# Real parts of eight squarings and the coefficient sums moved from VectorE to float32 matmuls with the identity

## The chip, the cores and the metric

The kernel runs on one core of one Trainium2 chip. The metric is the time of one execution on the device in microseconds (us). In the profile the engines are named PE (TensorE: matmuls; PEld: its weight loads), DVE (VectorE), ACT (ScalarE), POOL (GpSimd) and SP (SyncE, which here only issues DMAs). On each engine instructions run in the order in which the program lists them.

## The reference

Two layers, A and B, are applied twice in turn to one sequence of 2048 rows of 512 values (bfloat16), each on the normalised rows and with the input added back:

```python
x = A_x
x = x + _A_ref(_layernorm(x, axis=-1), A_wqkv, A_wo)
x = x + _B_ref(_layernorm(x, axis=-1), B_A_re, B_A_im, ...)
x = x + _A_ref(_layernorm(x, axis=-1), A_wqkv, A_wo)
x = x + _B_ref(_layernorm(x, axis=-1), B_A_re, B_A_im, ...)
```

A is attention with 32 heads of 16 over a window of 8 positions with step 2. B is a long convolution of every channel d with a filter K of 2048 taps, done with Fourier transforms. The filter is made from a diagonal state-space model with 128 states per channel:

```python
logdA = dt * A                 # A, Bc, Cc complex, [512, 128]; dt = exp(log_dt)
dB = dt * Bc
P = jnp.exp(logdA[:, :, None] * l[None, None, :])        # l = 0 .. 2047
K = jnp.einsum("dn,dnl,dn->dl", Cc, P, dB).real
```

The filter is the same for both B layers and is made once. This is the kernel generation, the part that is changed.

## The kernel before

The kernel generation is the function `k_gen`. States lie on the 128 partitions; the 512 channels lie along the free dimension, so that one real plane is a tile of 128 x 512 float32. It works with z = exp(dt A) and its powers z^(2^k):

- In the head, the six parameter arrays are loaded (`raw`), turned by PE into PSUM (`turned_by`, tiles `pt`, four of them in turn), and z is made as a real and an imaginary plane (`sq_z`).
- Eleven squarings (k = 0 to 10) give z^2 to z^2048. `square` (letter `s`, L1078) lets ACT square both planes into `ws`; `double` (L1082) lets DVE make the imaginary plane 2 re im; `differ` (L1085) lets DVE make the real plane by subtracting the two squares. Calls of `i` take `double` and `differ` in turn, k by k.
- `power` (`b`, L1096 and L1098) copies a power as bfloat16 into a table of factors: powers 3 to 7 into `Pw` (`pow_t`), the others into `Bt` (`B_t`). For powers 3 to 7 a further `b` writes the negated imaginary plane (L1102 on ACT, for power 5 L1104 on DVE), and `c` copies the real plane once more by DMA (`power_copy`, L1107).
- `c_part` (`C`) makes the coefficients C dB: for the real and for the imaginary plane two products (`t1`, `t2`) and their difference or sum, into `c0` (`c_t`), all on DVE (L1110).
- `b_part` (`M`) fills `B_t` by complex products on DVE: with 1536 or 1024 columns, and adds with 512. It needs the powers 0, 1, 2, 8, 9 and 10.
- `levels` (`T` and `U`) builds four chunks of a table `A_t` from the coefficients on DVE, in five levels of doubling size, level n with the power 3 + n; `T` makes chunks 0 and 2, `U` chunks 1 and 3, and `H` begins a chunk.
- `product` (`p`, L1268) multiplies `A_t` with `B_t` on PE, and ACT copies the result to `kgs` (`x`, L1276). After the last one, `k_store` writes the filter to device memory.

Woven into this is the front of the first attention layer: the loads of x (`d`), the statistics of its rows on ACT (`a`) and DVE (`3`), the normalising (`l`, `W`, `y`, `z`), the transposes on PE (`t`, L1196) with their copies on ACT (`e`), the projections on PE (`k`, `q`, L1206) with their copies on ACT (`K`, `Q`), and the first products of the logits (`X`, `Z`, `o`, `E`). `G` and `w` make the constants of the Fourier transforms and store them.

The order of all this is written out by hand: `ORDERK` is a text of 368 letters, and a loop takes the next call of the list that belongs to each letter. So the order of the letters is the order of each engine's instructions. The engine of some copies stands in `ENGK`. The other stages have texts of their own (`ORDER0`, `ORDERF`, `ORDER1`, `CORE0`, `CORE1`).

The framework adds the waits between engines from what the instructions read and write; tiles of a pool with several buffers are taken in turn, and a new one waits for the users of the old.

Of the kernel before, what the change touches and what calls it, by code (L numbers as in the profile page):

```python
# [20 lines left out]
P = 128  # L21
# [13 lines left out]
N = 128  # L35
# [8 lines left out]
DQT = 8  # L44
NQT = DQG // DQT
ORDERK = """
isCbCiCbsiMaiCCbsiMiGGsbcCbMaTMiiMisMbiMbsGbMiGbiMTbcsibTTaiTcbTsbMTiiGbTGGsTMGciaiMTGMcabMGMaTM
asaMMGMlalTiWMlaaiyTbayiyTMawaMytatMTelkaeMsqMkdliqMaMKMaMMqMqWMlbQQMMMqMyHykUUakpKkyyttkaxUUpKU
kaUUUUaqUUxeUQppqHkdxxKUqeQTkTaUTklqT3paTqlKWTkQTplqkyqx3Ty3QKxT3TTpqlkTpyyHqWEUxktQlKtkUzkekeTK
zUUUkkzkUztKkKtkkTUpexUUKUEkUkeUkUKpKUokxkpxpKUkUxxkqUKEpxoqkkUpUUxopXXXKQpZxxZZ  # L50
"""
ORDER0 = """
KD KA KA KA KD KA KD KA KD KA KD kA KA kD KA KD UA KD UA UA UD KA kA kD kA UD
UA UD UA kD kA kD u UD u u UA m m m UA u u UD u UA m kD UA kD UA m
m u UA u m kA u kD u m kD u kD kA kA yA m YA m yD u yA u m m m
u u yA m m u YA m yA w000D yD yA YD yA w010D YA yD yA
"""
LATE0 = "a s t g r b m"
ORDERF = """
yA h00 YA h01 v100A v110D h10 a0 z12A p0 z11A n0D h11 w001A w011A S a1 p1 T0 E01A z13A E00D n1G H2  # L60
P02 a2 P00 Q00 p2 T1 E10D E11D P01 P11 P12 n2D H3 a3 P13 T2 P10 E20D E21D P03 p3 P21 P22 n3D
P23 T3 E30D E31A P20 x1
"""
ORDER1 = """
UA UD UA UD UA UA UD UA UD UD u u m m u u m m UA u UA UD m UA u u
UD UA u m m u u m m u YD m u YA YA m u yD m yA u u m m u w001A
m m yA yA w000D YA yD yA YD w011D yA yD w010D yA yD yA v101A v103D v113A v102D v112D v111D v110A v100A
"""

CORE0 = """  # L70
# [914 lines left out]
NIA = 32  # L985
CH = 32
NROW = 641


def k_gen(tc, nc, a_consts, ins, kd, la, x_v, lnst, zero, b_consts):  # L990

    B_L = (0, 1, 2, 3, 4, 5, 6, 7, 256, 258, 260, 262, 512, 516, 768, 772, 1024, 1280, 1536, 1792, 2048)
    NCH = P // CH
    with ExitStack() as ctx:
        pw = ctx.enter_context(tc.tile_pool(name="kg_pow", bufs=1))
        Bt = pw.tile([P, 2, P, NB, 4], BF16, name="B_t")
        Pw = pw.tile([P, NCH, 5, 4, 4 * CH], BF16, name="pow_t")
        c0 = pw.tile([P, 2, 4 * P], BF16, name="c_t")
        tab = [ctx.enter_context(tc.tile_pool(name="kg_tab0", bufs=1))]
        c_psum, c_small = ExitStack(), ExitStack()  # L1000
        sp = c_small.enter_context(tc.tile_pool(name="kg_small", bufs=1))
        pst = c_psum.enter_context(tc.tile_pool(name="kg_ps_t", bufs=4, space=PSUM))
        late = {}
        iotas, a_rest = a_consts(sp)
        ident = la.c["ident"]
        la.front_open()
        la.front_psum()
        xb, ln, lvar, xps, pps = {}, {}, {}, {}, {}
# [10 lines left out]
        raw = {}  # L1019
        for name in ("A_im", "A_re", "B_re", "B_im", "C_re", "C_im"):  # L1020
            raw[name] = sp.tile([P, 4, N], BF16, name="raw_" + name)
            nc.sync.dma_start(raw[name][:], ins[name].rearrange("(t p) n -> p t n", p=P))
        x_load(0)
        zero()
        x_load(1)
# [29 lines left out]
        cur = {0: sp.tile([P, 2, 4 * P], F32, name="sq_z", tag="sq_z", bufs=2)}  # L1055
        a_re, turn = cur[0][:, 0], ws[:, 2]
# [12 lines left out]
        T = {name: turned_by(name, by_dt if name[0] == "C" else plain) for name in ("B_re", "B_im", "C_re", "C_im")}  # L1069
        for name, copy in (("B_re", nc.scalar.copy), ("B_im", nc.scalar.copy)):  # L1070
            b = sp.tile([P, 4 * P], BF16, name="in_" + name)
            copy(nat(b[:]), T[name])
            T[name] = nat(b[:])
        nc.vector.tensor_tensor(cur[0][:, 1], a_re, sn, ALU.mult)
        nc.vector.tensor_tensor(cur[0][:, 0], a_re, cs, ALU.mult)

        def square(k):
            nc.scalar.activation(ws[:, 0:2], cur[k][:], ACT.Square)  # L1078

        def double(k):  # L1080
            cur[k + 1] = sp.tile([P, 2, 4 * P], F32, name="sq_z", tag="sq_z", bufs=2)
            nc.vector.scalar_tensor_tensor(cur[k + 1][:, 1], cur[k][:, 0], 2.0, cur[k][:, 1], ALU.mult, ALU.mult)  # L1082

        def differ(k):
            nc.vector.tensor_tensor(cur[k + 1][:, 0], ws[:, 0], ws[:, 1], ALU.subtract)  # L1085

        def planes(k):
            return cur[k][:].rearrange("p r (c x) -> p r c x", c=NCH)

        def copy_by(eng):  # L1090
            return nc.scalar.copy if eng == "A" else nc.vector.tensor_copy

        def power(k):
            copy = copy_by(ENGK["b"][k + max(0, min(k - 3, 5))])
            if 3 <= k <= 7:
                copy(Pw[:, :, k - 3, 1::2, :].rearrange("p c r x -> p r c x"), planes(k))  # L1096
            else:
                copy(Bt[:, :, :, B_L.index(1 << k), :], cur[k][:].rearrange("p r (q g) -> p r q g", g=4))  # L1098

        def power_neg(k):  # L1100
            if ENGK["b"][2 * k - 2] == "A":
                nc.scalar.mul(Pw[:, :, k - 3, 2, :], planes(k)[:, 1], -1.0)  # L1102
            else:
                nc.vector.tensor_scalar(Pw[:, :, k - 3, 2, :], planes(k)[:, 1], -1.0, None, ALU.mult)  # L1104

        def power_copy(k):
            nc.sync.dma_start(Pw[:, :, k, 0, :], Pw[:, :, k, 1, :])  # L1107
# [1 line left out]
        def tt(*args):  # L1109
            return lambda: nc.vector.tensor_tensor(*args)  # L1110

        def c_part():
            for q, (x0, y0, x1, y1, op) in enumerate((("C_re", "B_re", "C_im", "B_im", ALU.subtract),
                                                      ("C_re", "B_im", "C_im", "B_re", ALU.add))):
                yield tt(nat(t1[:]), T[x0], T[y0], ALU.mult)
                yield tt(nat(t2[:]), T[x1], T[y1], ALU.mult)
                yield tt(c0[:, q], t1[:], t2[:], op)

        def bmul(src, by, dst):
            s0, s1, st = src  # L1120
# [258 lines left out]
def kernel(  # L1379
# [200 lines left out]
```

## Time and profile before

| | |
|---|---|
| median of 3 runs | 403.94 us (403.01 to 404.91) |
| span of the profiled execution | 402.6 us (its own time is not given) |
| DVE busy | 383.5 us, 95% of the span |
| PE busy (matmuls) | 328.0 us, 81% |
| ACT busy | 321.8 us, 80% |
| POOL busy | 59.1 us, 15% |
| DVE's last instruction of the kernel generation (L295) | ends at 110.7 us |
| k_store's 24 DMAs | issued from 110.01 us on |

The profile is of one execution; its span runs from the first instruction to the last. A row of the timeline has the start, the time, the engine, the line, the operation, the tile written, the tiles read and the shapes; in brackets stands how long the engine sat idle before, and what ended that. A row of the groups has the count, the busy time in us, the mean in ns and the idle time before. A row of a window has the length, the busy time of the engines with the number of instructions, the granted clock of TensorE, the share of time in which the DMA engines were busy, and GB/s. The two rows of digits show the span in 40 slices of 10.1 us, each digit the busy share in tenths.

### The profile page before, as it was taken

Reading aid. Unit: us, or ns where it says so; the run is one execution under the profiler, and the core shown is the slowest. Engines: PE = TensorE matmul, PEld = TensorE weight load, DVE = VectorE, ACT = ScalarE, POOL = GpSimd, SP = SyncE. Lnnn points to the kernel's source line nnn. Section 1 sums busy time; section 2 is a strip of 40 time slices with the busy share of each in tenths; the row PEclk is TensorE's granted clock in tenths of the full one; section 3 lists DMA queues with packets and bytes.
Section 4 is the critical chain, followed back from the end, with each engine's and each line's share of the span. In section 5 each row is a group of like instructions: output and inputs, shape, how many; then the busy total and the mean of one; then the engine's idle time right before and its main releaser. Section 6 shows DMA issues by size and latency. Waiting matters only on the chain.

```text
span 402.6 us, 14781 instructions
## 1 busy us (share of the span) xinstructions
PE 328.0 (81%) x6527; PEld 230.3 (57%) x6527; DVE 383.5 (95%) x460; ACT 321.8 (80%) x557; POOL 59.1 (15%) x75
## 2 busy tenths in 40 slices
PE   3000059999999989999998889999999998997895
PEld 2000026657735656756987888543456666566885
DVE  6999999999999999999999998979899999989994
ACT  7999888898656578988999987674666677989974
POOL 9402400000199500200600000100000001000000
PEclk9999997999999999999999999999999999999999
DMA  7952711115013875259236685730063019504606
GB/s 219 395 143 37 81 52 50 44 27 117 3 43 76 214 210 160 55 173 384 93 112 232 228 285 166 280 114 2 0 170 94 3 39 383 161 2 134 186 14 202
DMA packets 62323, 54.17 MB, mean 135 GB/s; under 512 B 33869, under 2 KB 50738, under 8 KB 60978
## 3 DMA queue, kind: packets, MB, share of 16 engines
q1 hardware_dynamic: 62250, 53.22, 43.5%
q8 instruction: 51, 0.84, 0.9%
q14 instruction: 14, 0.11, 0.1%
q10 hardware_dynamic: 8, 0.00, 0.0%
HBM read 30.15 MB, written 13.24 MB: 108 GB/s over the span
## 4 chain that ended last, share of the span: by engine, by line
PE 36%; DVE 31%; ACT 17%; issue 8%; DMA 5%; SPq 2%; POOL 1%; DVEq 0%; ACTq 0%; POOLq 0%
DVE pav L467 11%; PE pq L398 6%; PE pk L1268 5%; ACT a1s L791 5%; PE pp L1206 4%; DVE t L847 3%; PE pq L223 3%; DVE prod L342 3%; PE pp L282 3%; PE L L350 2%; ACT ub L860 2%; DVE B_t L1110 2%; DVE sq_z L1085 2%; DMA v_ext<-v_ext 2%; DMA kf_ring<-kf_dram 2%
## 5 line engine op out<-in xcount | busy, mean ns | idle before, releaser
L467 DVE TENSOR_TENSOR pav<-attn,v_ext 128x4096 bf16<-128x4096 bf16 (+1 forms) x34 | 72.4, 2168 | 0.4 <-DMA v_ext<-v_ext 0.3
L342 DVE TENSOR_TENSOR prod<-qT,kT_ext 128x4096 bf16<-128x4096 bf16 x29 | 67.0, 2341 | 1.4 <-PE L L350 0.9
L1196 PE MATMUL pt<-ident,x_blk 128*128 128x128 bf16 x64 | 5.9, 241 | 42.8 <-DVE x_blk L197 38.6
L1110 DVE TENSOR_TENSOR A_t<-A_t,pow_t 128x1024 bf16<-128x1024 bf16 (+4 forms) x46 | 38.3, 870 | 0.3
L492 PEld LDWEIGHTS <-pav 64*128 64x128 bf16 x1664 | 26.2, 95 | 13.5 <-DVE pav L467 8.6
L503 PE MATMUL pq<-wop,oT 128*128 128x512 bf16 x128 | 32.9, 379 | 0.7 <-ACT oT L494 0.7
L860 ACT CAST ub<-pb 128x1024 bf16<-128x1024 f32 x32 | 32.1, 1079 | 1.2 <-PE pb L809 1.2
L492 PE MATMUL po<-ident,pav 64*128 64x64 bf16 x1664 | 29.3, 190 | 4.2 <-DVE pav L467 3.2
L400 ACT CAST v_ext<-pq 128x512 bf16<-128x512 f32 x32 | 18.8, 586 | 16.2 <-PE pq L398 16.2
L809 PE MATMUL pb<-a1s,w_sb 128*128 128x64 bf16 x768 | 27.4, 193 | 5.0 <-ACT a1s L791 1.7
L398 PE MATMUL pq<-wv,xnT 128*128 128x512 bf16 x128 | 30.6, 380 | 0.0
L1206 PE MATMUL pp<-xnT,kT_ext 128*128 128x512 bf16 x96 | 27.1, 411 | 4.3 <-ACT kT_ext L1211 2.3
L1196 PEld LDWEIGHTS <-x_blk 128*128 128x128 bf16 x64 | 4.6, 107 | 44.8 <-DVE x_blk L197 38.8
L809 PEld LDWEIGHTS <-w_sb 128*128 128x128 bf16 x768 | 24.9, 98 | 7.2 <-issue 5.2
L791 ACT CAST a1s<-pb 128x1024 bf16<-128x1024 f32 x29 | 28.2, 1059 | 0.8 <-PE pb L802 0.8
L1268 PEld LDWEIGHTS <-A_t 128*64 128x64 bf16 (+1 forms) x512 | 22.9, 107 | 4.5 <-DVE B_t L1110 0.3
L1268 PE MATMUL pk<-B_t,A_t 128*64 128x84 bf16 (+1 forms) x512 | 24.6, 206 | 0.0
L791 DVE CAST a1s<-pb 128x1024 bf16<-128x1024 f32 x19 | 22.6, 1217 | 1.4 <-PE pb L802 1.3
L223 PE MATMUL pq<-xnT,kT_ext 128*128 128x512 bf16 x96 | 23.9, 380 | 0.0
L225 ACT CAST qT<-pq 128x512 bf16<-128x512 f32 x24 | 14.1, 586 | 9.3 <-PE pq L223 9.2
L509 ACT ACTIVATE x_sb<-pq 128x512 bf16<-128x512 f32 x24 | 14.3, 594 | 8.7 <-PE pq L503 8.7
L398 PEld LDWEIGHTS <-xnT 128*128 128x128 bf16 x128 | 11.6, 98 | 15.3 <-issue 3.0
(259 smaller groups left out, 897.0 us busy)
## 6 DMA issues: line engine op xcount, KB each, us to landing
w_sb<-w_dram SPq DMA_DIRECT2D x8, 1024.0 KB, 7.8
w_dram<-xnT SPq DMA_DIRECT2D x1, 4096.0 KB
kf_ring<-kf_dram SPq DMA_DIRECT2D x13, 256.0 KB, 4.8
kf_ring<-kf_dram SPq DMA_DIRECT2D x26, 128.0 KB, 4.3
v_ext<-v_ext SPq DMA_DIRECT2D x4, 784.0 KB, 6.6
x_blk<-in_A_x_dram SPq DMA_DIRECT2D x4, 512.0 KB, 4.1
kT_ext<-in_A_wqkv_dram SPq DMA_DIRECT2D x4, 512.0 KB, 9.2
x_sb<-in_A_x_dram SPq DMA_DIRECT2D x4, 512.0 KB, 5.3
```

The lines of the kernel that those rows point to most:

```text
L223: nc.tensor.matmul(pq[:], lhsT=self.wqk[:, dt, ft * P:(ft + 1) * P], rhs=self.xnT[:, dt, q * 512:(q + 1) * 512], start=(dt == 0), stop=(dt ...
L342: nc.vector.tensor_tensor(pr, self.qT[q][:, ft].unsqueeze(1).to_broadcast([P, W, 4, P]), kap, ALU.mult)
L398: nc.tensor.matmul(pp[:], lhsT=xnT[:, dt, a * P:(a + 1) * P], rhs=wv[:, dt, :], start=(dt == 0), stop=(dt == NDT - 1))
L467: nc.vector.tensor_tensor(pv[:, i], attn[:, n % 4].unsqueeze(2).to_broadcast([P, W, DH // parts, H]), vap, ALU.mult)
L492: nc.tensor.matmul(po[:, h, 0, i * nt + ft, :], lhsT=pvf[rows, i, w, ft * P:(ft + 1) * P], rhs=ident[rows, rows], start=(w == 0 and ft + i ...
L503: nc.tensor.matmul(pw[:], lhsT=oT[:, ftp, :], rhs=self.wo[:, ftp, :], start=False, stop=(ftp == NDT - 1))
L791: (self.nc.scalar.copy if eng == "act" else self.nc.vector.tensor_copy)(dst, src)
L809: nc.tensor.matmul(p2[:, j, :], lhsT=self.w2[:, ec * EC + j, :], rhs=a1s[:, ec * EC + j, :], start=True, stop=True)
L860: nc.scalar.copy(ub[:], p2)
L1110: return lambda: nc.vector.tensor_tensor(*args)
L1206: nc.tensor.matmul(pps[kind, b, ft][:], lhsT=la.wqk[:, dt, c:c + P], rhs=la.xnT[:, dt, b * 512:(b + 1) * 512], start=(dt == 0), stop=(dt = ...
L1268: nc.tensor.matmul(o, lhsT=lhs, rhs=Bt[:, ri, c * CH + ql].rearrange("p b g -> p (b g)"), start=(not half and j % 4 == 0 and ri == 0), sto ...
```

## The change

- `k_gen` makes two float32 identities, `ident32` and `nident32` (the negated one), from `ident` by DVE at its start.
- `differ` for k = 3 to 10 no longer runs on DVE: PE adds the two squares up in a PSUM tile by two float32 matmuls, one with the identity and one with the negated identity. The real plane of the powers 4 to 11 then stays in PSUM (a tile of the pool of `pt`) and is read from there by `square`, `double` and `power`. The imaginary plane has a tile of its own, so ACT's squares and power copies of k = 4 and up are made plane by plane, 512 columns each.
- The difference and the sum in `c_part` are made in the same way by PE, and copied to `c0` by ACT. The second pair of products has tiles of its own, in room of `kT` that is not yet used.
- The `raw` tiles lie in the room of `qT`.
- `ORDERK` has the same 368 letters in another order. The other order texts differ only in their line breaks.

The diff, cut to this:

```diff
+sibCCiisbisCCCiiMMbsGiCMMiMMbbMMsTbGiiscbbccMMbiTisbTTbGGGcGTTTiTTGiiTTTsGbibbGGGasTcMMMMaiiaaaa
+aasMMTiillWaTlbyMMwMyyayMMaMMMbattseeMMMiiMMMMkkMMMMMkkbKHqqKaqqppaaQadxaUUUUUUUkkllxUWppaQUUKlq
+UqyUUUqqyyHyQxttkkTTTTTpdeeKTTTTQT3qqqqaaQkkQaakkKTaallqxqpWEQx333KxlTTykkkppTkyyyxxHtUUeKUUtppl
+kUUeUKkxkkUWpUlzKzzzxkkttKkeKekpUUUUUKkkkkUUUEUUxUKEqxppKooxqXkxkQpKkkoXXKpZZZxx
...
+SQ_PE = 3
...
+        ident32 = sp.tile([P, P], F32, name="ident32")
+        nident32 = sp.tile([P, P], F32, name="nident32")
+        nc.vector.tensor_copy(ident32[:], ident[:])
+        nc.vector.tensor_scalar(nident32[:], ident[:], -1.0, None, ALU.mult)
...
         def square(k):
-            nc.scalar.activation(ws[:, 0:2], cur[k][:], ACT.Square)
+            if k <= SQ_PE:
+                nc.scalar.activation(ws[:, 0:2], (im[k] or z0)[:], ACT.Square)
+                return
+            for r in range(2):
+                nc.scalar.activation(ws[:, r], cur[k][r], ACT.Square)
 
         def double(k):
-            cur[k + 1] = sp.tile([P, 2, 4 * P], F32, name="sq_z", tag="sq_z", bufs=2)
-            nc.vector.scalar_tensor_tensor(cur[k + 1][:, 1], cur[k][:, 0], 2.0, cur[k][:, 1], ALU.mult, ALU.mult)
+            z = sp.tile([P, 1 if k >= SQ_PE else 2, 4 * P], F32, name="sq_z", tag=f"sq_z{k >= SQ_PE}", bufs=2)
+            nc.vector.scalar_tensor_tensor(z[:, 0 if k >= SQ_PE else 1], cur[k][0], 2.0, cur[k][1], ALU.mult, ALU.mult)
+            im[k + 1] = z
 
         def differ(k):
-            nc.vector.tensor_tensor(cur[k + 1][:, 0], ws[:, 0], ws[:, 1], ALU.subtract)
...
+            if k < SQ_PE:
+                cur[k + 1] = im[k + 1][:, 0], im[k + 1][:, 1]
+                nc.vector.tensor_tensor(cur[k + 1][0], ws[:, 0], ws[:, 1], ALU.subtract)
+                return
+            re = pst.tile([P, 4 * P], F32, name="pt")
+            nc.tensor.matmul(re[:], lhsT=ident32[:], rhs=ws[:, 0], start=True, stop=False)
+            nc.tensor.matmul(re[:], lhsT=nident32[:], rhs=ws[:, 1], start=False, stop=True)
+            cur[k + 1] = re[:], im[k + 1][:, 0]
...
+        def c_sum(q, t):
+            pc = pst.tile([P, 4 * P], F32, name="pt")
+            nc.tensor.matmul(pc[:], lhsT=ident32[:], rhs=t[0], start=True, stop=False)
+            nc.tensor.matmul(pc[:], lhsT=(ident32 if q else nident32)[:], rhs=t[1], start=False, stop=True)
+            nc.scalar.copy(c0[:, q], pc[:])
```

More of the change, by code (lines that the diff above doesn't have):

```diff
@@ L1019, in k_gen @@
         raw = {}
+        q0, q1 = (la.qT[b][:].rearrange("p t a q -> p (t a q)") for b in range(2))
         for name in ("A_im", "A_re", "B_re", "B_im", "C_re", "C_im"):
-            raw[name] = sp.tile([P, 4, N], BF16, name="raw_" + name)
-            nc.sync.dma_start(raw[name][:], ins[name].rearrange("(t p) n -> p t n", p=P))
+            home = (q0, q1)[len(raw) // 4]
+            raw[name] = home[:, len(raw) % 4 * 512:(len(raw) % 4 + 1) * 512].rearrange("p (t n) -> p t n", n=N)
+            nc.sync.dma_start(raw[name], ins[name].rearrange("(t p) n -> p t n", p=P))
         x_load(0)
@@ L1054, in k_gen @@
         t2 = sp.tile([P, 4 * P], F32, name="t2")
-        cur = {0: sp.tile([P, 2, 4 * P], F32, name="sq_z", tag="sq_z", bufs=2)}
-        a_re, turn = cur[0][:, 0], ws[:, 2]
+        z0 = sp.tile([P, 2, 4 * P], F32, name="sq_z", tag="sq_zFalse", bufs=2)
+        cur = {0: (z0[:, 0], z0[:, 1])}
+        a_re, turn = cur[0][0], ws[:, 2]
         p_im = turned_by("A_im", by_dt)
@@ L1094, in power @@
             copy = copy_by(ENGK["b"][k + max(0, min(k - 3, 5))])
[L1095 to L1098, printed above, removed]
+            if k <= SQ_PE:
+                z = (im[k] or z0)[:]
+                if k >= 3:
+                    copy(Pw[:, :, k - 3, 1::2, :].rearrange("p c r x -> p r c x"), z.rearrange("p r (c x) -> p r c x", c=NCH))
+                else:
+                    copy(Bt[:, :, :, B_L.index(1 << k), :], z.rearrange("p r (q g) -> p r q g", g=4))
+                return
+            for r, z in enumerate(cur[k]):
+                if 3 <= k <= 7:
+                    copy(Pw[:, :, k - 3, 1 + 2 * r, :], z.rearrange("p (c x) -> p c x", c=NCH))
+                else:
+                    copy(Bt[:, r, :, B_L.index(1 << k), :], z.rearrange("p (q g) -> p q g", g=4))
         def power_neg(k):
             if ENGK["b"][2 * k - 2] == "A":
-                nc.scalar.mul(Pw[:, :, k - 3, 2, :], planes(k)[:, 1], -1.0)
+                nc.scalar.mul(Pw[:, :, k - 3, 2, :], cur[k][1].rearrange("p (c x) -> p c x", c=NCH), -1.0)
             else:
-                nc.vector.tensor_scalar(Pw[:, :, k - 3, 2, :], planes(k)[:, 1], -1.0, None, ALU.mult)
+                nc.vector.tensor_scalar(Pw[:, :, k - 3, 2, :], cur[k][1].rearrange("p (c x) -> p c x", c=NCH), -1.0, None, ALU.mult)
         def power_copy(k):
@@ L1110, in tt @@
             return lambda: nc.vector.tensor_tensor(*args)
-        def c_part():
[L1113 to L1117, printed above, removed]
+        def c_sum(q, t):
[3 more added lines that the diff above has]
+            nc.scalar.copy(c0[:, q], pc[:])
+        prods = [(t1[:], t2[:]), [la.kT[:, 3, a:a + 8, :].rearrange("p a q -> p (a q)").bitcast(F32) for a in (14, 22)]]
+        def c_part():
+            for q, (x0, y0, x1, y1) in enumerate((("C_re", "B_re", "C_im", "B_im"), ("C_re", "B_im", "C_im", "B_re"))):
+                t = prods[q]
+                yield tt(nat(t[0]), T[x0], T[y0], ALU.mult)
+                yield tt(nat(t[1]), T[x1], T[y1], ALU.mult)
+                yield lambda: c_sum(q, t)
         def bmul(src, by, dst):
```

28 lines of the change are left out of this document (11 added, 17 removed).

## The prediction

> **What bounds the kernel now.** I read the page first, then the busy time by stretch, then the chain, then single rows.
>
> ```profile
> span 402.6 us, 14781 instructions
> PE 328.0 (81%) x6527; PEld 230.3 (57%) x6527; DVE 383.5 (95%) x460; ACT 321.8 (80%) x557; POOL 59.1 (15%) x75
> ...
> PE   3000059999999989999998889999999998997895
> ...
> DVE  6999999999999999999999998979899999989994
> ```
>
> ```profile
> 9.00:60.00 51.00, 6.65 (x28) 3.18 (x29) 50.70 (x83) 46.84 (x87) 12.05 (x14) 0.99 0.57 148
> 60.00:110.70 50.70, 48.57 (x663) 33.66 (x663) 49.41 (x72) 42.61 (x78) 1.15 (x3) 0.94 0.21 48
> ```
>
> The whole edit lies in the kernel generation, which holds VectorE (DVE) until 110.7 us. The second fence has, per stretch, its length and then the busy time of PE, PEld, DVE, ACT and POOL. From 9 to 60 us DVE is busy for 50.70 of 51.00 us and PE for 6.65: there a DVE instruction taken away shortens the stage, and PE has room. From 60 to 110.7 DVE (49.41) and PE (48.57) are both nearly full.
>
> ```profile
> 39.51 1.14 DVE A_t L1110
> 40.65 1.47 DVE B_t L1110 x2
> ...
> 103.65 1.40 PE pp L1206 x6
> 105.05 4.18 PE pk L1268 x96
> 109.23 0.98 PE L L350 x16
> ```
>
> The chain that ended last says the same: it runs over DVE's tables around 40 us and ends this stage on PE's products, which eat those tables. So a gain made on DVE early has to reach PE later.
>
> **What the change removes.**
>
> ```profile
> L1082 DVE SCALAR_TENSOR_TENSOR sq_z<-sq_z 128x512 f32<-128x512 f32 x11 | 7.7, 698 | 0.0
> L1085 DVE TENSOR_TENSOR sq_z<-ws 128x512 f32<-128x512 f32 x11 | 7.5, 683 | 0.1
> L1110 DVE TENSOR_TENSOR B_t<-B_t 128x1536 bf16<-128x1536 bf16 x4 | 3.8, 952 | 0.0
> L1110 DVE TENSOR_TENSOR A_t<-A_t,pow_t 128x2048 bf16<-128x2048 bf16 x2 | 2.4, 1215 | 0.0
> L1110 DVE TENSOR_TENSOR c_t<-t,t 128x512 bf16<-128x512 f32 x2 | 1.5, 728 | 0.0
> L1110 DVE TENSOR_TENSOR t<-pt,in_B_re 128x512 f32<-128x512 f32 x2 | 1.4, 679 | 0.0
> L1110 DVE TENSOR_TENSOR A_t<-A_t,pow_t 128x1024 bf16<-128x1024 bf16 x2 | 1.3, 685 | 0.0
> L1110 DVE TENSOR_TENSOR A_t<-A_t,pow_t 128x512 bf16<-128x512 bf16 x2 | 0.8, 419 | 0.0
> L1110 DVE TENSOR_TENSOR A_t<-A_t,pow_t 128x256 bf16<-128x256 bf16 x2 | 0.6, 284 | 0.0
> ```
>
> ```profile
> 22.31 0.68 DVE L1085 TENSOR_TENSOR sq_z<-ws 128x512 f32<-128x512 f32 x1
> 22.92 0.95 DVE L1110 TENSOR_TENSOR B_t<-B_t 128x1536 bf16<-128x1536 bf16 x1
> ```
>
> These are DVE's groups from 9 to 60 us, with the mean in ns after the comma. An instruction starts about 0.08 us before the one ahead of it has ended (22.31 + 0.68 against 22.92), so each costs its mean less 0.08 us. Of the eleven subtractions of L1085 eight go: 8 x 0.60 = 4.8 us. Both sums `c_t` go: 2 x 0.65 = 1.3 us. Together 6.1 us of DVE. The doublings (L1082) stay; eight of them now read one operand from PSUM, which I price at nothing: the products that read `pt` in PSUM take 679 ns, no more than the 698 of L1082 from SBUF.
>
> **What it adds in the head.** Two copies that widen the identity, on DVE.
>
> ```profile
> 1.21 0.56 POOL L92 TENSOR_SCALAR ident<-iota_id 128x128 bf16<-128x128 int32 x1
> ...
> 3.21 0.69 DVE L1045 TENSOR_TENSOR dt_diag<-ident,pt 128x512 bf16<-128x512 bf16 x1 [1.63 <-PE pt L1043]
> ```
>
> They wait for `ident` (done at 1.77 us) and stand ahead of `dt_diag`, for which DVE sat idle for 1.63 us until 3.21. The nearest row, 256 columns at 0.28 us, bounds the two at 0.56 us: hidden by that idle time, and 0.4 to 0.6 us on the path without it.
>
> **What it adds on ACT.** Squares and power copies of k = 4 and up are cut in two halves, and the two sums are copied out of PSUM.
>
> ```profile
> L1078 ACT ACTIVATE ws<-sq_z 128x1024 f32<-128x1024 f32 x11 | 11.5, 1048 | 0.0
> ...
> L1072 ACT CAST in_B_re<-pt 128x512 bf16<-128x512 f32 x1 | 0.6, 562 | 0.0
> ```
>
> A half takes 0.56 us and so some 0.48 us of the queue, the whole 1048 less 80 ns, 0.97: two halves cost no more than the whole, and only the two copies are new, 2 x 0.48 = 1 us. ACT had 4.2 us to spare before 60 us (46.84 of 51.00), and the new order moves the row statistics (`a`) behind the squarings. I take nothing for it.
>
> **What it adds on PE, and the new wait.** Twenty matmuls in float32, 512 columns wide, two for each real part (k = 3 to 10) and each sum. No row has a float32 matmul. The nearest are bf16 ones of that width:
>
> ```profile
> 60.96 2.72 PE L1206 MATMUL pp<-xnT,kT_ext 128*128 128x512 bf16 x6 [1.13 <-ACT qT L1211]
> 72.93 1.47 PE L1206 MATMUL pp<-xnT,kT_ext 128*128 128x512 bf16 x6
> ```
>
> ```profile
> L1206 PEld LDWEIGHTS <-kT_ext x96: 95/98/152, 53.0 to 104.5; 128*128 128x128 bf16 x96
> ```
>
> Six in 2.72 us are 0.425 us each and 0.17 at the end; six in 1.47 are 0.217. The same work at two clocks: half speed before 66 us, full speed after. Bounds for a float32 matmul: one such pass at the cheap end; at the dear end four (both operands have two halves, 2 x 2 products), each with its weight load of 0.098 us standing ahead of it rather than beside the matmul before, as it does in these rows. I take four passes with hidden loads: a pair costs 8 x 0.217 = 1.74 us at full clock and 8 x 0.425 = 3.40 at half. The Trainium skill (FP8 and Floating Point Precision, TensorE Precision Notes) gives four passes for true float32; by it the sum is the one taken; no trace here shows it.
>
> A squaring was a square on ACT and a subtraction on DVE; now the next one waits for a ring: half a square (0.57), the pair, and 0.25 us for the end of the matmul and the wake-up. That is 2.56 us at full clock and 4.22 at half. While DVE waits at a doubling, all tables behind it in its queue wait too. How long, follows from the new order text. From doubling 4 to the first `M` that needs power 8, DVE has these to do, by the rows above:
> - doubling 4, two `M` of 1536, the negated copy of power 5: 0.60 + 2 x 0.87 + 0.34 = 2.68
> - doubling 5, three `T` of 256 and three of 512: 0.60 + 3 x 0.20 + 3 x 0.34 = 2.22
> - doubling 6, two `T` of 1024: 1.80
> - doubling 7, one `T` of 1024, three of 2048: 0.60 + 0.60 + 3 x 1.13 = 4.59
>
> In all 11.29 us. Against them stand four rings (real parts 5 to 8), the copy of power 8 in two halves (1.04), and one more item, for which there is a row:
>
> ```profile
> 353.00 0.69 DVE L138 BATCH_NORM_STATS2 ln_bn<-pq 128x6 f32<-128x512 f32 x1
> 353.73 0.59 ACT L507 CAST x_sb<-pq 128x512 bf16<-128x512 f32 x1 [0.37 <-DVE ln_bn L138]
> ```
>
> Two engines that only read one PSUM tile were run one behind the other. Doubling 7 stands ahead of square 7 in the text and both read real part 7, now in PSUM, so this ring carries 0.69 us more. At full clock: 4 x 2.56 + 0.69 + 1.04 = 11.97, so DVE waits 0.68 us. At half: 4 x 4.22 + 1.73 = 18.61, it waits 7.32. For real part 4 DVE has 4.9 us of work against a ring of 4.7 at half clock, in PE's queue behind the second sum: 0.4 us. Behind doubling 8 the slots (4.5 us, 9.5 us) hold a ring at either clock.
>
> SP's queue keeps its order (five power copies, the stores, the loads), and POOL's work isn't moved. But a `T` level also waits for the DMA copy of its power:
>
> ```profile
> pow_t<-pow_t SPq DMA_DIRECT2D x5, 128.0 KB, 3.2
> ```
>
> That is 3.2 us from issue to landing, behind ACT's power copy, so at full clock a `T` level can be late by about what a ring is. It runs beside the ring that DVE waits for next, so I add nothing for it; it could keep 0.5 us.
>
> So the clock decides, and it has rows (length, PE's busy time, granted clock):
>
> ```profile
> 52.45:55.87 3.42, 3.17 (x15) 1.00 0.40 108
> 55.87:59.28 3.41, 1.40 (x8) 1.00 0.11 46
> 59.28:62.69 3.41, 2.28 (x7) 0.50 0.00 0
> 62.69:66.10 3.41, 3.41 (x36) 0.50 0.02 5
> ```
>
> ```profile
> 369.86:373.27 3.41, 2.01 (x63) 1.00 0.67 192
> ```
>
> After a stretch with 3.17 of 3.42 us busy the clock was full; after one with 1.40 it was lost; 2.28 didn't bring it back, 3.41 did; 2.01 of 3.41 later kept it. (The 1.00 shown before 55.87 is no measurement: matmuls there run at the half-speed pitch.) In the new order the two sums and real part 4 feed PE almost without a gap from some 10.5 us on, three pairs of 3.40, so full clock should come by 18 us. From then PE works 1.74 us in each 2.56, 68%, between the 59% that kept the clock and, where ACT's power copies stretch a ring to 4 us, the 41% that lost it. I take three rings at full clock and one at half: 1.66 us more.
>
> **The sum.** -6.1 + 0.4 + 0.7 + 1.7 = -3.3 us at the end of the stage. Behind 110.7 us no instruction changes, and the next stage starts from what ends here on DVE, PE and ACT, so I let the shift carry through: the profiled span of 402.6 becomes 399.3. The profiled execution's own time isn't given; its span lies 1.3 us below the median of 403.94, and I keep that: 400.6 us.
>
> **The rivals.**
>
> Full clock through all rings: -6.1 + 0.4 + 0.7 = -5.0, 398.9 us. For it, the 59% that kept the clock; against it, the 41% row. The Trainium skill (TensorE: Matmul & The Clock Gate, HAM oscillation) has it that only gaps of PE over about 3.4 us cost the clock, and a ring leaves 0.8 us, so by this rule the rival holds. The trace speaks against the rule: the clock went at 59.28 though PE's longest gap in that stretch was 2.0 us.
>
> ```profile
> 58.59 1.24 PE L1206 MATMUL pp<-xnT,kT_ext 128*128 128x512 bf16 x4 [2.01 <-ACT kT_ext L1211]
> ```
>
> Slower: the squarings on PE become the bound, at doublings 5 to 8, because the clock stays at half there. The waits eat the 6.1 us as soon as a ring is longer than (11.29 + 5.7 - 1.73) / 4 = 3.8 us. With hidden loads (ring 4.22) the sum is -6.1 + 0.4 + 7.3 = +1.6; with the loads ahead of each pass a pair is 8 x 0.523 = 4.18, the ring 5.0, the wait 10.4 and the sum +4.7. Middle: +3.2, 407.1 us. For it: PE has been idle for tens of us in this stretch before, and it took a nearly full 3.4 us to raise the clock.
>
> Given back: DVE's 3 us come early but PE's stretch from 90 to 110 us, where the chain is PE's alone, doesn't move. Then 403.9 us, no change. Against it: PE was idle for 2.1 of 50.7 us from 60 on and for 44 before, and 5 us of that stretch ran at half clock.
>
> The dear and the cheap end of the matmul at full clock are -1.9 (ring 3.34, wait 3.8) and, with one pass, -5.7: both within the range.
>
> **How the numbers follow.** Forecast 0.45 (one or two rings at half clock, -1.6 to -4.0), full clock 0.17, slower 0.26, given back 0.12. A measurement of this kernel can tell about 0.5%, 2.0 us, from no change. Faster by more: most of the forecast (0.35) and the full clock, 0.52. Slower by more: the dearer two thirds to three quarters of that rival, 0.20. Within: the rest, 0.28. The range reaches from 398.4, just under the full clock, to 406.8, near the middle of the slower rival, which leaves out some 0.13 above and 0.05 below.
>
> **What would show it.** In the profile after: DVE's subtractions at 512 columns fall from eleven to three; twenty float32 matmuls, or their passes, between 10 and 60 us, a pair in 1.7 or 3.4 us; DVE's idle time there put down to PE or to ACT's squares, around doublings 5 to 8, at 1 to 3 us in all; the last product of the stage (`pk`, at 109.2 us before) some 3 us earlier, and the same shift at the end. I am wrong if the pair takes over 3.4 us at full clock, if the granted clock or the pitch stays at half through all rings, if the statistics or the copies on ACT hold the rings instead, or if the stage ends earlier and the kernel doesn't.

## The result and the profile after

The changed kernel took 400.51 us (median of 6 runs, 399.46 to 401.65). The kernel before took 404.0 (6 runs, 402.97 to 405.03). The ratio is 0.9916, with a 95% interval of 0.9892 to 0.9941: faster by some 3.4 us. The forecast was 400.6. That it came so close is partly luck: in its sum one term was too large by 1.7 us and a term of 2.2 us was missing, so that the two nearly cancelled, and at the end of the stage only 2.06 of the 3.3 us that were forecast had been gained. The rest came further down, where the prediction had put no change.

The profiled execution took 401.65 us, as long as any of the six, with a span of 399.9 us. So 1.75 us lie around a span, not the 1.3 that I had taken. Its page:

```profile
span 399.9 us, 14829 instructions
...
PE 347.0 (87%) x6519; PEld 237.1 (59%) x6567; DVE 378.8 (95%) x452; ACT 323.6 (81%) x574; POOL 53.6 (13%) x75
...
PE   3755489799999979889997899999999998897995
```

PE's row has new digits where it had zeros, from 10 to 50 us. DVE has 4.7 us less work (378.8 against 383.5) and eight instructions fewer. Busy time by stretch, with the columns as before:

```profile
9.00:60.00 51.00, 32.31 (x67) 11.55 (x69) 48.83 (x78) 46.33 (x93) 7.01 (x14) 0.80 0.57 149
60.00:110.00 50.00, 46.52 (x666) 32.67 (x674) 47.76 (x68) 45.46 (x90) 2.37 (x3) 1.00 0.22 50
```

DVE, which had 0.30 us to spare from 9 to 60 us, now has 2.17. What it waits for between 9 and 100 us is the whole of this answer (waits of DVE, by line and releaser):

```profile
DVE ln_veps L1202 <- ACT ln_junk L144: 0.9, 1, 0.9
DVE sq_z L1094 <- ACT ws L1090: 0.7, 1, 0.7
DVE B_t L1135 <- ACT B_t L1123: 0.4, 1, 0.4
DVE sq_z L1100 <- ACT ws L1087: 0.3, 1, 0.3
DVE A_t L1135 <- ACT A_t L1260: 0.2, 1, 0.2
```

DVE's groups show the removal as forecast, three subtractions (L1100) for eleven; seven of the doublings (L1094), not eight, read PSUM, at the old price:

```profile
L1094 DVE SCALAR_TENSOR_TENSOR sq_z<-pt,sq_z 128x512 f32<-128x512 f32 x7 | 4.8, 684 | 0.7 <-ACT ws L1090 0.7
...
L1100 DVE TENSOR_TENSOR sq_z<-ws 128x512 f32<-128x512 f32 x3 | 2.1, 711 | 0.3 <-ACT ws L1087 0.3
```

PE's matmuls with the identities (timeline; each is recorded as two, hence x2): the first sum, real part 4, real part 7 and real part 8.

```profile
10.53 2.07 PE L1139 MATMUL pt<-t,ident 128*128 128x512 f32 x2 [2.60 <-DVE t L1135]
12.40 1.82 PE L1140 MATMUL pt<-t,nident 128*128 128x512 f32 x2
...
17.12 1.12 PE L1103 MATMUL pt<-ws,ident 128*128 128x512 f32 x2 [0.84 <-ACT ws L1087]
18.08 1.02 PE L1104 MATMUL pt<-ws,nident 128*128 128x512 f32 x2
...
25.69 1.13 PE L1103 MATMUL pt<-ws,ident 128*128 128x512 f32 x2 [0.69 <-ACT ws L1090]
26.66 1.02 PE L1104 MATMUL pt<-ws,nident 128*128 128x512 f32 x2
30.60 1.65 PE L1103 MATMUL pt<-ws,ident 128*128 128x512 f32 x2 [2.92 <-ACT ws L1090]
32.04 1.91 PE L1104 MATMUL pt<-ws,nident 128*128 128x512 f32 x2
```

The second matmul starts 0.96 us after the first at full clock (17.12 to 18.08) and 1.87 at half (10.53 to 12.40). Real parts 5, 6 and 7 were made at full clock, 8 at half: three and one, as forecast. PE's clock in these windows (length, busy time of PE, PEld, DVE, ACT, POOL, then the granted clock):

```profile
27.56:30.97 3.41, 0.49 (x2) 0.30 (x2) 3.38 (x6) 2.53 (x9) 0.00 (x0) 1.00 0.18 41
30.97:34.38 3.41, 2.98 (x4) 0.67 (x2) 3.17 (x3) 2.21 (x6) 0.00 (x0) 0.51 0.17 38
34.38:37.80 3.42, 0.36 (x1) 0.30 (x2) 3.19 (x4) 3.42 (x10) 1.43 (x3) 0.99 0.13 14
```

Here the window with 0.49 of 3.41 us busy was followed by one at half clock, and the window with 2.98 by one at full clock.

To see where DVE's time went I take one fixed place in its stream: the third product of the logits (`A_pr`), behind all tables. In the kernel before and in the changed one it is

```profile
107.81 2.28 DVE L342 TENSOR_TENSOR A_pr<-qT,kT_ext 128x4096 bf16<-128x4096 bf16 x1
```

```profile
105.75 2.29 DVE L341 TENSOR_TENSOR A_pr<-qT,kT_ext 128x4096 bf16<-128x4096 bf16 x1
```

so 2.06 us earlier. The table splits this, for every kernel that ran. I add up DVE's instructions from the doubling at 9.17 us to this product, one by one: their durations; the overlaps and small gaps between neighbours (an instruction that starts before the one ahead has ended counts below zero); and the waits, which are gaps over 0.115 us. In brackets stands the number of instructions that start no earlier than 0.03 us before the end of the one ahead.

| kernel | durations | neighbours | waits | third `A_pr` | ratio to the kernel before (95%) |
|---|---|---|---|---|---|
| before | 107.64 | -9.76 (20) | 0.75 | 107.81 | |
| changed | 100.87 | -6.78 (36) | 2.48 | 105.75 | 0.9916 (0.9892 to 0.9941) |
| order alone | 107.88 | -7.68 (38) | 0.30 | 109.67 | 1.0040 (1.0015 to 1.0065) |
| old order | 100.96 | -8.28 (23) | 10.30 | 112.14 | 1.0181 (1.0146 to 1.0217) |
| sums only | 106.52 | -7.63 (37) | 0.30 | 108.35 | 0.9993 (0.9982 to 1.0003) |
| squarings only | 102.26 | -6.96 (37) | 3.30 | 107.76 | 0.9983 (0.9957 to 1.0009) |
| squarings, PE kept busy | 101.97 | -7.00 (36) | 0.95 | 105.08 | 0.9949 (0.9923 to 0.9975) |
| clock kept | 100.81 | -7.01 (36) | 1.17 | 104.12 | 0.9911 (0.9881 to 0.9941) |
| bf16 pairs | 100.83 | -6.92 (37) | 0.30 | 103.37 | 0.9891 (0.9862 to 0.9919) |
| pairs doubled | 100.90 | -6.47 (36) | 8.10 | 111.71 | 1.0103 (1.0081 to 1.0124) |
| neighbours split | 100.81 | -7.89 (25) | 2.46 | 104.56 | 0.9960 (0.9938 to 0.9981) |
| clock and neighbours | 100.72 | -7.70 (26) | 2.54 | 104.72 | 0.9903 (0.9884 to 0.9922) |

From before to changed: -6.77 of durations, +2.98 at the neighbours, +1.73 of waits. Ten instructions that are gone take some 0.08 us of overlap each with them, 0.8; so the pure removal is worth 6.0 us, and 2.2 us are lost at neighbours for another reason. The prediction has no term for that.

### The profile page after: what moved, and what is told of

Same layout as the page of the kernel before. It is cut to its first block, busy times and chain, and to the rows that moved or that the text cites. A ratio compares the mean times of both kernels' runs of the same rounds, so it can differ in the third digit from the quotient of the medians.

```text
span 399.9 us, 14829 instructions
## 1 busy us (share of the span) xinstructions
PE 347.0 (87%) x6519; PEld 237.1 (59%) x6567; DVE 378.8 (95%) x452; ACT 323.6 (81%) x574; POOL 53.6 (13%) x75
## 4 chain that ended last, share of the span: by engine, by line
PE 39%; DVE 33%; ACT 15%; issue 6%; DMA 4%; SPq 1%; ACTq 0%; DVEq 0%
DVE pav L466 9%; PE pq L397 7%; DVE A_t L1135 6%; DVE t L846 4%; PE pq L222 4%; DVE prod L341 3%; PE pp L281 3%; PE pk L1301 3%; PE pp L1239 3%; PE pb L808 2%; PE L L349 2%; ACT a1s L790 2%; DMA w_sb<-w_dram 2%; ACT ln_junk L144 2%; PE po L491 2%
## 5 line engine op out<-in xcount | busy, mean ns | idle before, releaser
L502 PE MATMUL pq<-wop,oT 128*128 128x512 bf16 x123 | 31.9, 379 | 3.8 <-issue 2.5
L1301 PEld LDWEIGHTS <-A_t 128*64 128x64 bf16 (+1 forms) x512 | 21.7, 103 | 5.6 <-issue 1.2
L1301 PE MATMUL pk<-B_t,A_t 128*64 128x84 bf16 (+1 forms) x512 | 23.6, 201 | 1.6 <-ACT kgs L1309 1.0
L1239 PE MATMUL pp<-xnT,kT_ext 128*128 128x512 bf16 x87 | 23.2, 390 | 1.5 <-ACT kT_ext L1244 0.4
L222 PE MATMUL pq<-xnT,kT_ext 128*128 128x512 bf16 x91 | 23.1, 379 | 0.4 <-issue 0.2
L1103 PE MATMUL pt<-ws,ident 128*128 128x512 f32 x16 | 11.0, 778 | 13.8 <-ACT ws L1090 12.9
L502 PEld LDWEIGHTS <-oT 128*128 128x128 bf16 x128 | 12.3, 98 | 13.3 <-ACT oT L493 1.3
```

Source lines behind the costliest of these rows:

```text
L222: nc.tensor.matmul(pq[:], lhsT=self.wqk[:, dt, ft * P:(ft + 1) * P], rhs=self.xnT[:, dt, q * 512:(q + 1) * 512], start=(dt == 0), stop=(dt ...
L502: nc.tensor.matmul(pw[:], lhsT=oT[:, ftp, :], rhs=self.wo[:, ftp, :], start=False, stop=(ftp == NDT - 1))
L1239: nc.tensor.matmul(pps[kind, b, ft][:], lhsT=la.wqk[:, dt, c:c + P], rhs=la.xnT[:, dt, b * 512:(b + 1) * 512], start=(dt == 0), stop=(dt = ...
L1301: nc.tensor.matmul(o, lhsT=lhs, rhs=Bt[:, ri, c * CH + ql].rearrange("p b g -> p (b g)"), start=(not half and j % 4 == 0 and ri == 0), sto ...
```

## The experiments

**The order alone, and the operations alone.** The kernel before with the new order text, and the changed kernel with the old one:

```diff
 # order alone: the kernel before
-isCbCiCbsiMaiCCbsiMiGGsbcCbMaTMiiMisMbiMbsGbMiGbiMTbcsibTTaiTcbTsbMTiiGbTGGsTMGciaiMTGMcabMGMaTM
+sibCCiisbisCCCiiMMbsGiCMMiMMbbMMsTbGiiscbbccMMbiTisbTTbGGGcGTTTiTTGiiTTTsGbibbGGGasTcMMMMaiiaaaa
...
 # old order: the changed kernel
-sibCCiisbisCCCiiMMbsGiCMMiMMbbMMsTbGiiscbbccMMbiTisbTTbGGGcGTTTiTTGiiTTTsGbibbGGGasTcMMMMaiiaaaa
+isCbCiCbsiMaiCCbsiMiGGsbcCbMaTMiiMisMbiMbsGbMiGbiMTbcsibTTaiTcbTsbMTiiGbTGGsTMGciaiMTGMcabMGMaTM
...
```

> The kernel before with the new ORDERK alone: subtractions and sums stay on VectorE, no float32 matmul. Theory A (the prediction): the change takes 6.1 us of VectorE work away and loses 2.8 us of it to waits for real parts made by PE, 1.7 of them for the one ring at half clock; so with the old operations the new order gives back 6.1 and loses no 2.8: about 403.8 us, as before. Theory B (from the two traces): the waits for real parts are only some 0.4 us; the rest that is missing, 1.7 us, is lost because the new order puts more instructions right behind the one they depend on (33 such neighbours on VectorE up to the end of the tables instead of 19, each about 0.12 us dearer than independent neighbours), and 0.9 on statistics; so the order alone is slower than before: 405 to 406 us. Rival C: the new order itself is the gain: 400.5 us.

> The changed kernel with the ORDERK of before: the new operations in the old order. Theory: the new order costs by itself (405.7 against 404.1 us) and is what the float32 pairs need. In the old order ACT's copies of the coefficient sums stand ahead of the copies of powers 1 and 2 that VectorE needs, each behind a float32 pair of 3.7 us, and the doublings 5 to 9 come 2.0 to 3.2 us apart, against rings of 2.7 us at full clock; some 6 us of waits at the head and some 4 to 6 at the rings against 6.1 us of work saved: 408 to 413 us. Rival: the old order serves as well, and the operations alone make the gain: 399 to 401 us.

The order alone took 405.72 us (before: 404.06): slower by 0.15 to 0.65%. By the table it removes a wait (0.75 to 0.30) and loses 2.08 us at the neighbours. There the count in brackets goes from 20 to 38. DVE's timeline shows what stands in it. In the kernel before:

```profile
27.06 0.28 DVE L1110 TENSOR_TENSOR A_t<-A_t,pow_t 128x256 bf16<-128x256 bf16 x1
27.26 0.68 DVE L1082 SCALAR_TENSOR_TENSOR sq_z<-sq_z 128x512 f32<-128x512 f32 x1
27.87 0.28 DVE L1110 TENSOR_TENSOR A_t<-A_t,pow_t 128x256 bf16<-128x256 bf16 x1
```

and in the changed one:

```profile
25.44 0.49 DVE L1135 TENSOR_TENSOR A_t<-A_t,pow_t 128x256 bf16<-128x256 bf16 x2
25.97 0.29 DVE L1135 TENSOR_TENSOR A_t<-A_t,A_t 128x256 bf16<-128x256 bf16 x1
...
27.43 0.69 DVE L1094 SCALAR_TENSOR_TENSOR sq_z<-pt,sq_z 128x512 f32<-128x512 f32 x1
```

Before, a doubling stands between two steps of a table level, and each starts 0.07 to 0.08 us before the end of the one ahead. After, the three steps of a level stand one behind the other (`T` `T` `T`), and the one that adds the two products starts 0.04 us after their end (25.44 + 0.49 = 25.93, then 25.97). The two kinds don't mix: up to the third `A_pr` of the changed kernel 100 instructions start 0.06 to 0.10 us before the end of the one ahead, and the 36 in brackets 0.03 to 0.11 us after it. So a step that reads what the instruction ahead has just written is some 0.12 us dearer, and sixteen to eighteen more of them are about 2 us.

The old order under the new operations took 411.63 us, slower by 1.5 to 2.2%, with 10.3 us of waits. The two dearest rows of its timeline are in the head:

```profile
15.90 0.69 DVE L1135 TENSOR_TENSOR B_t<-B_t 128x1024 bf16<-128x1024 bf16 x1 [3.41 <-ACT B_t L1117]
...
23.44 0.24 DVE L1260 COPY A_t<-c_t 128x256 bf16<-128x256 bf16 x1 [2.56 <-ACT c_t L1141]
```

So the order is no gain of its own; it costs 1.9 us at the third `A_pr` and buys room for the new rings, 10.3 us of waits down to 2.48.

**One part of the operations at a time**, in the new order: only the two sums on PE (`SQ_PE = 11`), or only the squarings.

```diff
 # sums only
-SQ_PE = 3
+SQ_PE = 11
...
 # squarings only
-                yield lambda: c_sum(q, t)
+                yield tt(c0[:, q], t[0], t[1], ALU.add if q else ALU.subtract)
```

> The changed kernel with all squarings as before on VectorE and ACT (whole squares and copies too); only the two coefficient sums stay on PE, in the new order. If each instruction taken off VectorE is worth its 0.65 us: 1.3 us less than the new order alone (405.7), 404.4 us.

> The changed kernel with the two coefficient sums back on VectorE; only the real parts of eight squarings on PE. If each instruction taken off VectorE is worth its 0.65 us: 1.3 us more than the changed kernel (400.5), 401.8 us. As PE has less to do ahead of real part 4, the clock may rise later; if the rings then run at half clock, 403 us or more.

They took 403.86 and 403.58 us (before: 404.28); neither can be told from no change. Against the order alone, the sums bring the third `A_pr` 1.32 us forward (109.67 to 108.35), just the 1.3 of the prediction. The squarings bring 1.91, though 5.6 us of durations are gone: they wait 3.30 us. Together that would be 3.23, but the changed kernel has 3.92. The squarings alone wait 3.30 us, the changed kernel 2.48, and the largest of their waits is one that the changed kernel doesn't have (timeline of the squarings alone, PE and DVE):

```profile
17.70 2.07 PE L1103 MATMUL pt<-ws,ident 128*128 128x512 f32 x2 [10.41 <-ACT ws L1087]
19.57 1.92 PE L1104 MATMUL pt<-ws,nident 128*128 128x512 f32 x2
22.23 2.07 PE L1103 MATMUL pt<-ws,ident 128*128 128x512 f32 x2 [0.75 <-ACT ws L1090]
...
28.19 0.69 DVE L1094 SCALAR_TENSOR_TENSOR sq_z<-pt,sq_z 128x512 f32<-128x512 f32 x1 [2.07 <-ACT pow_t L1121]
```

Without the sums PE had been idle for 10.41 us before real part 4, so 4 and 5 are made at half clock, and the doubling waits 2.07 us. That reading was tested by giving PE other work in place of the sums:

```diff
 # the squarings alone, PE kept busy; results of the 30 matmuls unused
+                    if q == 0:
+                        pw = la.ps_pj.tile([P, 512], F32, name="pp", tag=la.pj_tag)
+                        la.warm(pw, 30, dtd[:].rearrange("p t q -> p (t q)"))
```

> The kernel with the squarings alone on PE (sums on DVE), plus 30 bf16 matmuls of 512 columns with unused results on PE where the first sum stood in the changed kernel, so that PE is busy from about 7.5 to 16 us. If the 2.07 us that DVE waits at the doubling of power 5 in the squarings alone come from PE's clock, not yet raised when real parts 4 and 5 are made, the pairs of these fall from 3.8 to 1.9 us, the wait goes, the first logit product comes from 103.36 to about 101.3 us and the time to 401 to 402.5. If they come from something else (ACT's queue, the copies of powers), the wait stays at about 2 us and the time at 403 to 404.

It took 401.72 us (before: 404.49); the interval of its ratio overlaps that of the squarings alone, so it is the trace that decides. In its timeline the pairs of 4 and 5 run at full clock:

```profile
17.70 1.13 PE L1103 MATMUL pt<-ws,ident 128*128 128x512 f32 x2 [2.73 <-ACT ws L1087]
...
20.43 1.13 PE L1103 MATMUL pt<-ws,ident 128*128 128x512 f32 x2 [0.75 <-ACT ws L1090]
```

The 2.07 us are gone and the third `A_pr` moves from 107.76 to 105.08; the other 0.6 us of that are 0.28 less of the wait for the row statistics, 0.29 less of durations and 0.04 of overlaps. So the two sums do two things: they take 1.3 us from DVE, and they raise the clock for the squarings behind them.

**The price of a ring**, from both sides. Clock kept: matmuls with unused results after the pairs of real parts 7, 8 and 9. One pass: squares from k = 3 on in bfloat16, so that a pair is two plain matmuls; this makes the powers less exact. Pairs doubled: four float32 matmuls for a real part in place of two.

```diff
 # clock kept
+WARM = {6: 11, 7: 18, 8: 14}
...
+            if k in WARM:
+                pw = la.ps_pj.tile([P, 512], F32, name="pp", tag=la.pj_tag)
+                la.warm(pw, WARM[k], dtd[:].rearrange("p t q -> p (t q)"))
 # bf16 pairs: squares of k >= 3 go to this tile, and are read from it
+        wh = sp.tile([P, 2, 4 * P], BF16, name="wh")
 # pairs doubled: behind the first matmul
+            nc.tensor.matmul(re[:], lhsT=ident32[:], rhs=ws[:, 0], start=False, stop=False)
+            nc.tensor.matmul(re[:], lhsT=nident32[:], rhs=ws[:, 0], start=False, stop=False)
```

> The changed kernel with 11, 18 and 14 bf16 matmuls of 512 columns, whose result nobody reads, behind the pairs for real parts 7, 8 and 9, so that PE stays busy and keeps full clock. Pairs for real parts 8 and 9 then take 1.9 us instead of 3.6. Theory A: the ring at half clock costs 1.7 us, so 398.8 us. Theory B: VectorE waited only 0.44 us for power 8, so 400.1 us, within the noise of 400.5. If PE were late for its own work by the added matmuls, slower than 400.5.

> The changed kernel with the squares of k = 3 to 10 written as bfloat16 and added up by bf16 matmuls with the bf16 identities: one pass, 0.22 to 0.43 us each instead of 0.96 to 1.87 (the powers get less exact). The two coefficient sums stay float32. Theory A: all waits for real parts vanish, 0.4 + 0.7 + 1.7 us: 397.7 us. Theory B: only the 0.44 us for power 8 and a little for square 9 vanish: 399.9 us.

> The changed kernel with four float32 matmuls for each real part instead of two (the first square is added a second time and taken off again). A ring at full clock is then 0.57 + 3.85 + 0.25 = 4.7 us, over the 3.8 us from which the prediction's rival has the squarings as the bound. By the prediction's formula VectorE waits 4 x 4.67 + 1.73 - 11.29 = 9.1 us instead of 2.4, less a lead of 3 us that real part 4 has in the trace: 4 to 7 us slower than the changed kernel, 404.5 to 407.5. If the rings were covered by other work instead, 400.5 to 402.

With the clock kept the third `A_pr` comes at 104.12, 1.63 us earlier than in the changed kernel; the waits of `sq_z` and `B_t` on the squarings are gone, and what is left is 0.30 us in the head and 0.87 for the row statistics. The edit holds the clock for three pairs, those of real parts 8, 9 and 10, so the 1.63 us aren't the price of one ring. The kernel took 400.44 us, which can't be told from the changed one: in its trace the lead is gone further down (DVE's shift against the kernel before is 3.16 us there from 326 to 390 us, 3.25 in the changed kernel). What the clock is worth at the end of the kernel is therefore not shown. With one pass it is 103.37, the time 399.65: the lowest of all, though its interval overlaps that of the changed kernel. With doubled pairs DVE waits 8.10 us, about 6 of them at doublings and at the first `M` of power 8, and the time is 407.98, just above the range expected. That is the slower rival made real: its rings at full clock last 4.38 us (pairs start at 21.56 and 25.94), about what one at half clock does (4.53 in the squarings alone, 17.70 to 22.23).

**Neighbours kept apart.** The letters of `T`, `U` and `M` moved so that fewer dependent steps stand one behind the other; then the same with the clock kept.

```diff
-sibCCiisbisCCCiiMMbsGiCMMiMMbbMMsTbGiiscbbccMMbiTisbTTbGGGcGTTTiTTGiiTTTsGbibbGGGasTcMMMMaiiaaaa
+sibCCiisbisCCCiibsGMMiMCibbMsbTGMMMMiiscMbTbccbTiisTbbGTGTcMGiGiTisGTbiTbTTTbGGGaMsMMcaMiTiaTaa
...
```

> The changed kernel with the letters T, U and M alone moved by some places, so that fewer VectorE instructions stand right behind the one that they depend on (some 10 fewer such neighbours); all operations are the same. Theory A knows no such cost: 400.5 us. Theory B: 10 x 0.12 = 1.2 us less, and up to 1.5 us more where the moves also fill the waits for power 8 and for the row statistics: 398.0 to 399.4 us.

> The changed kernel with two edits that were tried singly: the order with dependent DVE instructions kept apart, and the matmuls on PE (11, 18 and 14, results unused) that hold its clock. Alone, the order brought the first logit product to 98.95 us and the clock to 99.72, against 101.34 for the changed kernel. Theory A (they take different stalls away and the shift carries through): product at 97.3 to 98.9 us, time 397.5 to 399.0. Theory B (what starts earlier is taken back further down, by the idle time of PE at its instruction supply that the order alone showed, 2.3 us at 239 us): product as in A, time 399.5 to 402.

The neighbours' cost fell by 1.11 us (bracket 36 to 25), and the third `A_pr` came 1.19 us earlier: the mechanism is there, in the expected size. Yet the time was 402.15 us, no less than that of the changed kernel and longer than either theory had it. With the clock kept too it was 400.54, in the range of theory B, though the third `A_pr` came 1.03 us earlier than in the changed kernel. Two things took from the gain. First, the moved steps wait elsewhere (waits of DVE in the kernel with both edits):

```profile
DVE A_t L1139 <- DMA pow_t<-pow_t: 1.2, 1, 1.2
DVE A_pr L341 <- ACT kT_ext L294: 0.9, 1, 0.9
```

A table step now comes up before the DMA copy of its power has landed, and the tables are done before ACT has copied what the logits read. (The first `A_pr`, at 99.10 us there, has two table steps behind it; that is why I compare at the third. My expectation for the kernel with both edits took the first, and that made the new order look better than it is.) Second, in the profile of the order without the clock edit, PE stood still far down the kernel:

```profile
241.26 0.22 PE L873 MATMUL pb<-Wp,t 128*128 128x128 bf16 x1 [2.30 <-issue]
```

It waited for nothing that the profile shows (that it waited for instructions, as my expectation has it, is not shown), and 2.1 us of the shift went there. With both edits this idle time did not occur. The squarings alone have one of 1.64 us at the same line, the old order one of 2.1; the changed kernel has none. Its cause stays open, and so does whether it is in every execution of these kernels.

## Why the prediction was right, and which steps were not

- **Removed: 6.1 us.** Measured 6.0 (6.77 of durations less 0.8 of overlap), and for the sums by themselves 1.32 against 1.3.
- **The head.** The two copies lie in DVE's idle time there, and `dt_diag` starts at 3.22 as before, at 3.21 then:

```profile
1.79 0.56 DVE L1008 CAST ident<-ident 128x128 f32<-128x128 bf16 x1 [0.22 <-POOL ident L91]
1.93 0.48 DVE L1009 TENSOR_SCALAR nident<-ident 128x128 f32<-128x128 bf16 x1
...
3.22 0.69 DVE L1051 TENSOR_TENSOR dt_diag<-ident,pt 128x512 bf16<-128x512 bf16 x1 [0.81 <-PE pt L1049]
```

- **The float32 matmul.** Four passes at 0.217 and 0.425 us gave pairs of 1.74 and 3.40. Measured: 2 x 0.96 = 1.92 and 2 x 1.87 = 3.74, so 10% over the hidden-load price and far under the 4.18 with loads in the open at half clock. The four passes that the Trainium skill gives (FP8 and Floating Point Precision, TensorE Precision Notes) agree with 0.96 / 0.217 = 4.4, but for those 10%. A whole ring at full clock was forecast at 2.56 us; the pairs of real parts 5, 6 and 7 start 2.73 and 2.67 us apart (20.29, 23.02 and 25.69).
- **The clock.** Full well before 18 us, three rings at full and one at half: as forecast. The reason was another: I had expected ACT's power copies to stretch a ring, and it was DVE (next point). The half-clock ring was priced at 1.66 us. Its pair took 3.35 us (30.60 to 33.95) in place of the 1.99 of real part 7, 1.36 more, but DVE had other work meanwhile and waited 0.44 for power 8. The gap that lost the clock was 2.92 us long. By the Trainium skill (TensorE: Matmul & The Clock Gate, HAM oscillation) only longer gaps, over about 3.4 us, should do so; here the trace speaks against that rule as a limit, and with it against the rival "full clock through all rings".
- **The waits: 0.4 + 0.7 + 1.7 = 2.8 us.** This term failed. The waits on the squarings are 0.44 + 0.66 = 1.10 us; the 0.30 in the head belongs to the order, which has it alone too. The 0.4 for real part 4 was not worked out: 4.9 us of work against a ring of 4.7 leave nothing to wait for, unless PE is late from the second sum. It was not, its pair for real part 4 waited for ACT (17.12), and doubling 4 did not wait. For the rest, I had set four rings against the time from doubling 4 to the first `M` of power 8. But real part 5 needs nothing of doubling 4, and its pair started 1.9 us before that doubling:

```profile
20.29 1.12 PE L1103 MATMUL pt<-ws,ident 128*128 128x512 f32 x2 [1.19 <-ACT ws L1090]
```

```profile
22.17 0.68 DVE L1094 SCALAR_TENSOR_TENSOR sq_z<-pt,sq_z 128x512 f32<-128x512 f32 x1
```

 So the chain was ahead of DVE at doublings 5, 6 and 7, which never waited. From there it was the other way round: ACT's square of real part 7 waited for DVE, since doubling 7 read the same PSUM tile first.

```profile
29.95 0.60 ACT L1090 ACTIVATE ws<-pt 128x512 f32<-128x512 f32 x1 [0.88 <-DVE sq_z L1094]
```

 That item of the ring was named (0.69 us), and its further effect was not: it gave PE the 2.92 us gap. What was left are two waits:

```profile
34.61 0.96 DVE L1135 TENSOR_TENSOR B_t<-B_t 128x1536 bf16<-128x1536 bf16 x1 [0.44 <-ACT B_t L1123]
...
43.56 0.69 DVE L1094 SCALAR_TENSOR_TENSOR sq_z<-pt,sq_z 128x512 f32<-128x512 f32 x1 [0.66 <-ACT ws L1090]
```

 The first is behind the pair at half clock: ACT's copy of power 8 had to wait for it. The second is only indirectly PE's. PE had finished real part 9 at 40.79, but ACT's square of it started at 42.95, since ACT's queue was full of row statistics until then, and doubling 9 had to wait for that square.

```profile
33.99 0.59 ACT L1123 CAST B_t<-pt 128x512 bf16<-128x512 f32 x1 [1.20 <-PE pt L1104]
...
42.95 0.58 ACT L1090 ACTIVATE ws<-pt 128x512 f32<-128x512 f32 x1
```

 With the clock kept, ACT doesn't wait the 1.20 us, starts the same square at 41.61, and doubling 9 no longer waits. One sign that I had named for being wrong, the statistics on ACT holding a ring, so came true for this one.
- **Missing: the order's own price.** Every DVE instruction was priced at its mean less 0.08 us, whatever stood ahead of it. In the new order that is untrue for sixteen more of them: 2.2 us. The order alone shows it (2.08).
- **The sum at the stage's end.** Forecast -3.3, measured -2.06: 1.7 us less of waits on the squarings, 2.2 more at the neighbours, 0.6 of other waits (0.30 in the head, 0.16 for a copy of ACT, 0.18 more for the row statistics), and 0.1 less removed.
- **Carried through.** Roughly. In DVE's stream the shift is 2.06 us at the third `A_pr`, 2.35 at 127 us, 2.85 at 278, 3.25 from 326 to 390, and 2.31 at the end, where one residual addition waits 0.95 us longer for PE. The spans differ by 2.7 us, the medians by 3.5, and no execution of the changed kernel took longer than the profiled one; so the medians agree with the forecast of 3.3 better than the trace does. About half of the growth from 2.06 to 3.25 is no merit of the new operations: the order alone and the sums alone gain some 0.6 us over the same distance (the order alone is 1.86 us late at the third `A_pr` and 1.23 from 326 us on). Where that comes from, the new order or the one profiled execution of the kernel before, is open.
- **The rivals.** Slower (+1.6 to +4.7): its mechanism is real, as the doubled pairs show (407.98 us against 404.28, 0.8 to 1.2%), but the rings weren't that long. Given back: no; PE's products did start earlier. The first product behind the last `pk` began at 107.24 against 109.16, so 1.9 us earlier and not the 3 that I had named. Before and after:

```profile
105.83 3.39 PE L1268 MATMUL pk<-B_t,A_t 128*64 128x84 bf16 x74
109.16 1.05 PE L350 MATMUL L<-A_pr,ind 128*32 128x512 bf16 x16
```

```profile
105.83 1.48 PE L1301 MATMUL pk<-B_t,A_t 128*128 128x84 bf16 x32
107.24 1.05 PE L349 MATMUL L<-A_pr,ind 128*32 128x512 bf16 x16
```

## What to carry to other kernels

When work goes from a full engine to one that idles, price the latency of the ring that it joins and the clock at which the idle engine will run: here the two small sums ahead of the squarings saved their own 1.3 us and also raised the clock for what followed. When an order is rewritten, count which instructions now stand right behind the one whose result they read; on VectorE that cost 2.2 us here, over a third of what the change removed. And compare variants at an instruction behind all moved work, since one that only stands earlier in the text makes a gain that isn't there; then look at the end of the kernel too, where some of these gains were gone.

## What I had not expected of the hardware

- A VectorE instruction that read the result of the one ahead started about 0.04 us after its end, an independent one about 0.08 before it: 0.12 us, on instructions of 0.3 to 0.7 us (20 and 130 instructions in the kernel before, 36 and 100 in the changed one).
- In these traces the granted clock changed in steps of 3.41 us (30.97 and 34.38 in the changed kernel, 59.28 and 66.10 in the one before, which are two steps apart), and the steps of two traces lay differently: 59.28 and 30.97 are 8.3 steps apart. So one gap can fall differently in two executions. A gap of 2.92 us lost the clock in the changed kernel, with 0.49 us busy in its window; in the squarings with PE kept busy a gap of 3.03 did not, spread over windows with 1.98 and 1.52 us busy:

```profile
31.78 1.12 PE L1103 MATMUL pt<-ws,ident 128*128 128x512 f32 x2 [3.03 <-ACT ws L1090]
32.74 1.02 PE L1104 MATMUL pt<-ws,nident 128*128 128x512 f32 x2
```

 The squarings alone spread from 400.93 to 405.77 us (12 runs), the sums alone from 403.39 to 404.09 (12 runs), and the kernel before, beside them, from 403.08 to 405.76 (23 runs). Whether the place of the steps is what spreads them was not tested.
- The kernel with bf16 pairs ran with a mean granted clock of 0.63 from 9 to 60 us and still had the lowest median: DVE's only wait from 9 to 100 us was the 0.30 in the head, so at half clock too its rings were short enough.
